# Spreading the next segment's projections over all head groups, with PSUM evictions moved from VectorE to ScalarE

## The chip, the cores and the metric

The kernel runs on one core of a Trainium2 chip. The metric is device time in microseconds. Five engines work side by side, each through its own list of instructions in order: TensorE (PE: matmuls, and PEld: its weight loads), VectorE (DVE), ScalarE (ACT), GpSimd (POOL) and SyncE (SP, which here only starts transfers). Matmul results land in PSUM, eight banks of 2 KB per partition, from which DVE or ACT must copy ("evict") them to SBUF before the bank can be used again.

## The reference

The input x has 2048 rows of 640 numbers, and 32 heads of 20 columns. Two attention layers read the same x, and a gate per row mixes them:

```
A: q,k,v = x@wqkv;  pq = q@w_phi, pk = k@w_phi              (per head)
   phi_q = [softmax(pq), softmax(-pq)],  phi_k likewise
   a = (phi_q @ (phi_k^T v)) / (phi_q . sum(phi_k) + 1e-6) @ wo
B: q,k,v = x@wq, x@wk, x@wv, cut into 4 segments of 512 rows
   per segment s: p = softmax(q k^T / sqrt(20) + causal mask); dot = p @ v
                  mem = (phi(q) @ M) / (phi(q) . z + 1e-6)    phi(t) = t+1 if t>0 else exp(t)
                  o = sigmoid(beta)*mem + (1-sigmoid(beta))*dot
                  M += phi(k)^T v;  z += sum(phi(k))
   b = o @ wo
out = sigmoid(x . gate_w) * a + (1 - that) * b
```

All inputs and the output are bf16. Segment s of B reads the memory M that the segments before it have written; inside a segment only 512 x 512 causal scores per head are made.

## The kernel before

**Stages.** (1) Weights and x are loaded, x is transposed into xT. (2) Stage A1, 16 chunks of 128 rows: project k and v of layer A, exp with both signs (Ek), reduce, normalise (EkSn), transpose EkSn into PSUM (zt_ps, one tile per sign, two slots) and copy both tiles to ztsb. The first copy is on DVE (line 222), the second on ACT (line 223). DVE then adds up zacc from ztsb, 32 small additions for every four chunks. (3) A2 builds the key-value matrices of layer A. (4) A3 computes layer A's queries and output into oA. (5) Stage B, lines 405 to 647, which the change rewrites. The A stages other than line 222 are untouched.

**Stage B.** The loops run over 4 segments (s) and in each over 8 groups (g) of 4 heads. Four heads of 20 columns, padded to 32 each, fill the 128 partitions. For each segment there is a set of three tiles, phik, vB and kpad, in a pool of two sets. `alloc_seg_tiles` takes a set and zeroes its padding with four memsets on DVE (lines 420 to 423); it is called at the start of segment s for segment s+1, so four times in all.

`emit_b1` (line 426) fills a quarter of a set, one chunk of 128 rows: 20 matmuls into four PSUM tiles `proj` (k in two halves, v in two halves), two exps on ACT into ek, then on DVE a minimum, two copies to kpad (445), two combinations into phik (447) and two copies to vB (453).

A group does the following. `emit_proj` makes qT (5 matmuls, eviction on DVE) and, from segment 1 on, phiq (exp eq on ACT). `emit_kT` transposes kpad. `emit_qk` is called four times, c = 0 to 3: four matmuls into st_ps, one exp on ACT over 4 x (512 - 128 c) columns into PT (498), a mask on DVE (499). `emit_pv` multiplies PT with vB into nd_ps, `emit_mem` does the memory read and update, `emit_epi` normalises and writes oB. The source order is software-pipelined inside a segment: while group g makes its scores, the qT and kT of group g+1 and the rest (`prev`) of group g-1 are done.

Filler is emitted between groups: in groups 4 to 7 one whole `emit_b1` for the next segment per group, and from segment 1 on the output product of the segment before, one chunk of rows per two groups (`final_part1`, ten transposes, in even groups; `final_part2`, twenty matmuls o_ps, in odd ones). At the end of each segment the last group is finished (mem, pv, epi) before the next segment's memsets, first qT and first kT are emitted. The last segment's four output chunks come after everything.

**PSUM in B.** st_ps has one tile of four banks, nd_ps one bank, and one tag, ps1, has three slots of a bank each for all the rest: proj, qT_ps, kT_ps, amS, Mz, ndS, otp and o_ps.

**What sets the order.** Each engine executes a list in fixed order. The list is not quite the order of the source: a planner goes through the emitted instructions, takes those emitted earlier first where they are ready by its estimate, and inserts the waits. So the source order acts as a priority.

Of the kernel before, what the change touches and what calls it, by code (L numbers as in the profile page):

```python
# [7 lines left out]
ACT = mybir.ActivationFunctionType  # L8
# [7 lines left out]
def kernel(  # L16
# [16 lines left out]
    P = 128  # L33
# [145 lines left out]
    with tc.tile_pool(name="a1work", bufs=2, side="right") as a1w, \  # L179
# [4 lines left out]
        for sc in range(NCH):  # L184
# [37 lines left out]
            nc.vector.tensor_copy(out=ztsb[0:ZR, 0, :, sc % 4, :], in_=zts[0][0:ZR])  # L222
# [182 lines left out]
    with ExitStack() as bctx:  # L405
# [4 lines left out]
        bseg = bctx.enter_context(tc.tile_pool(name="bseg", bufs=2))  # L410
# [4 lines left out]

        def alloc_seg_tiles():
            phik = bseg.tile([P, 4, H, 32], BF16, name="phik")
            vB = bseg.tile([P, 4, H, 32], BF16, name="vB")
            kpad = bseg.tile([P, 4, H, 32], BF16, name="kpad")
            nc.vector.memset(kpad[:, :, :, DH:32], 0.0)  # L420
            nc.vector.memset(phik[:, :, :, DH:32], 0.0)
            nc.vector.memset(vB[:, :, :, DH + 1:32], 0.0)
            nc.vector.memset(vB[:, :, :, DH:DH + 1], 1.0)
            return phik, vB, kpad

        def emit_b1(tiles, sc, c):
            phik, vB, kpad = tiles
            pss = []
            for (Wr, lo) in ((None, 0), (None, 16), (WvB, 0), (WvB, 320)):
                ps = bps.tile([P, 320], F32, name="proj", tag="ps1")  # L430
                for cc in range(KC):
                    if Wr is None:
                        rhs = WkB[:, cc, lo * DH:(lo + 16) * DH]
                    else:
                        rhs = Wr[:, cc, lo:lo + 320]
                    nc.tensor.matmul(ps[:, 0:320], lhsT=xT[:, cc, sc * P:(sc + 1) * P], rhs=rhs,  # L436
                                     start=(cc == 0), stop=(cc == KC - 1))
                pss.append(ps)
            k0, k1, v0, v1 = pss
            ek = bw.tile([P, 2, 320], BF16, name="ek", tag="ek")  # L440
            nc.scalar.activation(out=ek[:, 0, :], in_=k0[:, 0:320], func=ACT.Exp)
            nc.scalar.activation(out=ek[:, 1, :], in_=k1[:, 0:320], func=ACT.Exp)
            nc.vector.tensor_scalar_min(out=ek, in0=ek, scalar1=1.0)
            for half, kp, vp in ((0, k0, v0), (1, k1, v1)):
                nc.vector.tensor_copy(out=kpad[:, c, half * 16:(half + 1) * 16, 0:DH],  # L445
                                      in_=kp[:, 0:320].rearrange("p (h d) -> p h d", d=DH))
                nc.vector.scalar_tensor_tensor(
                    out=phik[:, c, half * 16:(half + 1) * 16, 0:DH],
                    in0=kpad[:, c, half * 16:(half + 1) * 16, 0:DH],
                    scalar=0.0,  # L450
                    in1=ek[:, half, :].rearrange("p (h d) -> p h d", d=DH),
                    op0=ALU.max, op1=ALU.add)
                nc.vector.tensor_copy(out=vB[:, c, half * 16:(half + 1) * 16, 0:DH],
                                      in_=vp[:, 0:320].rearrange("p (h d) -> p h d", d=DH))

        seg_tiles = alloc_seg_tiles()
        for c in range(4):
            emit_b1(seg_tiles, c, c)
        for s in range(NSEG):
            phik, vB, kpad = seg_tiles  # L460
            nxt_tiles = alloc_seg_tiles() if s + 1 < NSEG else None
            def emit_proj(g):
                qT_ps = bps.tile([P, L], F32, name="qT_ps", tag="ps1")
                for cc in range(KC):
# [210 lines left out]
```

The softmax here doesn't subtract the row's maximum and nothing guards it: scores larger than these inputs give would overflow.

## Time and profile before

| | |
|---|---|
| runs | 578.66, 579.18, 574.02, 579.85 us; median 578.92 |
| profiled execution | 578.66 us, span of its instructions 576.9 us |
| mean granted TensorE clock | 0.893 |
| stage A1 (about) | 43 to 127 us of the span |
| opening of B, four chunks of proj | 224 to 242 us |
| segments 0, 1, 2, 3 of B, from first exp to first exp | 244.3, 322.6, 406.8, 492.3, end 556.5 us |
| tail | 556.5 to 576.9 us |

How to read it: a profile row "L498 ACT ACTIVATE PT<-st_ps ... x128 | 158.3, 1237 | 82.7 <-PE st_ps L494 81.5" is line 498 of the kernel, its engine, what it writes and reads, how often; then busy time in us and the mean duration of one in ns; then the idle time of that engine just before these instructions, and which instruction ended most of it. The chain of waits follows the work back from the last instruction, at each step to whatever released it. Durations overlap a little at their ends, so a sum of durations is slightly more than the time taken. "PEclk" is the TensorE clock that was granted, as a share of full speed.

### The profile page before, as it was taken

To read this page: it belongs to the slowest core of one execution; us is meant where nothing else is said; L and a number is where in the kernel's file an instruction comes from. 1 tells how busy PE (TensorE), PEld (TensorE's weight loads), DVE (VectorE), ACT (ScalarE), POOL (GpSimd) and SP (SyncE) were. 2 spreads that over 40 slices of the span, in tenths; PEclk is the share of its full clock that TensorE was granted. 3 is DMA by queue.
4 is the path that set the end of the run, shared out by engine and by line. 5 is a ranking of instruction groups with operands and counts; after the bars stand their busy time and mean duration, and the time that the engine had idled before them with its cause. 6 is when DMAs were issued, how large, how long until landed. Compare 5 with 4: busy or idle time off the path is not lost.

```text
span 576.9 us, 10001 instructions
## 1 busy us (share of the span) xinstructions
PE 450.3 (78%) x4021; PEld 269.5 (47%) x4054; DVE 430.7 (75%) x1186; ACT 306.8 (53%) x460; POOL 20.0 (3%) x24
## 2 busy tenths in 40 slices
PE   0798988956759985867878687887778888778887
PEld 0676765455435553533344343544343455344444
DVE  2379999999298879854587877867875878787841
ACT  1556766910535550255574567463676554677731
POOL 3020000000260000000000000000000000000000
PEclk9999997967998895967688999989997899799989
DMA  8300000000710000000000000000000000000001
GB/s 257 97 2 1 3 0 1 1 1 1 230 58 1 1 2 1 0 1 2 1 1 1 0 13 12 1 13 12 1 12 13 1 12 12 1 12 12 12 13 45
DMA packets 9045, 12.46 MB, mean 22 GB/s; under 512 B 1992, under 2 KB 8264, under 8 KB 9000
## 3 DMA queue, kind: packets, MB, share of 16 engines
q1 hardware_dynamic: 8056, 8.06, 4.3%
q0 software_dynamic: 800, 3.77, 1.9%
q8 instruction: 31, 0.51, 0.4%
q14 instruction: 14, 0.11, 0.1%
q10 hardware_dynamic: 144, 0.01, 0.0%
HBM read 9.21 MB, written 2.62 MB: 21 GB/s over the span
## 4 chain that ended last, share of the span: by engine, by line
DVE 42%; PE 40%; ACT 11%; issue 4%; DMA 3%; SPq 0%; ACTq 0%; DVEq 0%
PE o_ps L598 9%; PE proj L436 8%; ACT PT L498 7%; PE st_ps L494 5%; DVE zacc L230 4%; PE pq_ps L335 4%; DVE ndsb L520 3%; DVE PT L499 3%; DVE EkSn L203 3%; PE nd_ps L513 3%; PE qT_ps L465 3%; DVE ksum L199 3%; DMA wnat_k<-in_A_wqkv_dram 3%; PE ndS L561 2%; DVE qT L469 2%
## 5 line engine op out<-in xcount | busy, mean ns | idle before, releaser
L498 ACT ACTIVATE PT<-st_ps 128x2048 bf16<-128x2048 f32 (+3 forms) x128 | 158.3, 1237 | 82.7 <-PE st_ps L494 81.5
L499 DVE TENSOR_TENSOR PT<-PT,maskT 128x512 bf16<-128x512 bf16 x128 | 53.6, 420 | 31.3 <-ACT PT L498 30.1
L494 PE MATMUL st_ps<-qT,kT 32*128 32x256 bf16 (+3 forms) x512 | 49.0, 324 | 24.1 <-ACT PT L498 22.7
L513 PE MATMUL nd_ps<-PT,vB 128*32 128x256 bf16 (+3 forms) x512 | 46.4, 320 | 6.2 <-DVE PT L499 5.8
L494 PEld LDWEIGHTS <-kT 32*128 32x128 bf16 x512 | 18.4, 92 | 65.1 <-issue 60.8
L465 PE MATMUL qT_ps<-xT,WqB 128*128 128x512 bf16 x136 | 42.2, 402 | 7.5 <-DVE kT L486 2.0
L436 PEld LDWEIGHTS <-xT 128*128 128x128 bf16 x320 | 33.0, 110 | 26.8 <-issue 7.5
L335 PE MATMUL pq_ps<-xT,WqA 128*128 128x512 bf16 x153 | 40.1, 402 | 3.5 <-ACT dens L351 1.6
L338 ACT ACTIVATE Eq<-pq_ps 128x512 bf16<-128x512 f32 x32 | 19.1, 597 | 43.2 <-PE pq_ps L335 42.4
L598 PEld LDWEIGHTS <-oT 128*128 128x128 bf16 x320 | 32.6, 109 | 19.8 <-DVE oT L587 2.6
L189 PEld LDWEIGHTS <-xT 128*128 128x128 bf16 x320 | 31.6, 100 | 14.7 <-issue 2.1
L436 PE MATMUL proj<-WkB,xT 128*128 128x320 bf16 x160 | 33.1, 360 | 4.4 <-issue 4.1
L469 DVE CAST qT<-qT_ps 128x512 bf16<-128x512 f32 x32 | 22.3, 698 | 18.5 <-PE qT_ps L465 18.3
L598 PE MATMUL o_ps<-WoA,oT 128*128 128x320 bf16 x160 | 33.9, 344 | 1.4 <-DVE oT L587 1.4
L561 PE MATMUL ndS<-ident_b,ndsb 128*128 128x128 bf16 x128 | 14.9, 248 | 24.5 <-DVE ndsb L520 24.5
L230 DVE TENSOR_TENSOR zacc<-zacc,ztsb 80x256 bf16<-80x256 bf16 x128 | 31.0, 275 | 1.6 <-ACT ztsb L223 1.0
L598 PE MATMUL o_ps<-WoB,oT 128*128 128x320 bf16 x160 | 31.2, 331 | 0.2 <-DVE oT L587 0.2
L602 ACT CAST osb<-o_ps 128x320 bf16<-128x320 f32 x32 | 13.6, 424 | 32.6 <-PE o_ps L598 32.6
L436 PE MATMUL proj<-WvB,xT 128*128 128x320 bf16 x160 | 29.7, 327 | 1.0 <-DVE kpad L445 1.0
L520 DVE CAST ndsb<-nd_ps 128x512 bf16<-128x512 f32 x32 | 21.9, 686 | 9.9 <-PE nd_ps L513 9.6
L389 DVE TENSOR_TENSOR t<-num_ps,cs 128x480 f32<-128x480 f32 (+1 forms) x64 | 27.9, 473 | 0.3 <-PE num_ps L361 0.3
L513 PEld LDWEIGHTS <-vB 128*32 128x32 bf16 x512 | 19.2, 98 | 17.8 <-issue 8.9
(135 smaller groups left out, 822.1 us busy)
## 6 DMA issues: line engine op xcount, KB each, us to landing
out_dram<-osb SPq DMA_DIRECT2D x16, 160.0 KB, 1.8
x_nat<-in_A_x_dram POOLq DMA_DIRECT2D x1, 1280.0 KB, 11.3
x_nat<-in_A_x_dram SPq DMA_DIRECT2D x1, 1280.0 KB, 14.7
WvA<-in_A_wqkv_dram SPq DMA_DIRECT2D x1, 800.0 KB
wnat_k<-in_A_wqkv_dram SPq DMA_DIRECT2D x1, 800.0 KB, 14.9
wnat_q<-in_A_wqkv_dram POOLq DMA_DIRECT2D x1, 800.0 KB, 12.5
WoB<-in_B_wo_dram POOLq DMA_DIRECT2D x1, 800.0 KB, 5.4
wst<-in_B_wv_dram POOLq DMA_DIRECT2D x1, 800.0 KB, 7.5
```

The costliest lines, as they stand in the source:

```text
L189: nc.tensor.matmul(ps, lhsT=xT[:, c, sc * P:(sc + 1) * P], rhs=W[:, c, lo:hi], start=(c == 0), stop=(c == KC - 1))
L230: nc.vector.tensor_tensor(out=zacc[0:ZR, b4], in0=zacc[0:ZR, b4], in1=zt_tile[0:ZR, :, :, :, 4 * t:4 * t + 4], op=ALU.add)
L335: nc.tensor.matmul(pq_ps, lhsT=WqA[:, c, g * P:(g + 1) * P], rhs=xT[:, c, qt * L:(qt + 1) * L], start=(c == 0), stop=(c == KC - 1))
L436: nc.tensor.matmul(ps[:, 0:320], lhsT=xT[:, cc, sc * P:(sc + 1) * P], rhs=rhs, start=(cc == 0), stop=(cc == KC - 1))
L465: nc.tensor.matmul(qT_ps, lhsT=WqB[:, cc, 4 * g:4 * g + 4, :], rhs=xT[:, cc, s * L:(s + 1) * L], start=(cc == 0), stop=(cc == KC - 1))
L469: nc.vector.tensor_copy(out=qT, in_=qT_ps)
L494: nc.tensor.matmul(st_ps[:, i, 0:N], lhsT=kT[32 * i:32 * i + 32, c * P:(c + 1) * P], rhs=qT[32 * i:32 * i + 32, c * P:L], start=True, stop ...
L498: nc.scalar.activation(out=PT, in_=st_ps[:, :, 0:N], func=ACT.Exp, scale=SCALE_B)
L499: nc.vector.tensor_tensor(out=PT[:, :, 0:P], in0=PT[:, :, 0:P], in1=maskT[:, None, :].to_broadcast([P, 4, P]), op=ALU.mult)
L513: nc.tensor.matmul(nd_ps[32 * i:32 * i + 32, c * P:L], lhsT=vB[:, c, h, :], rhs=PTs[c][:, i, :], start=(c == 0), stop=(c == 3), tile_posit ...
L520: nc.vector.tensor_copy(out=ndsb, in_=nd_ps)
L598: nc.tensor.matmul(o_ps, lhsT=oTs[X][:, k5, :], rhs=Wo[:, k5, half * 320:(half + 1) * 320], start=(n == 0), stop=(n == 2 * KC - 1))
```

## The change

1. In A1 the first ztsb copy (line 222) goes from DVE to ACT, so both are on ACT.
2. In B, kpad and vB are evicted by ACT instead of DVE, in `emit_b1`. The function now can do one half of k or of v alone; the minimum and the two phik combinations stay on DVE and come with the second half of k.
3. Two sets of phik, vB and kpad are allocated and zeroed once, ahead of the first `emit_b1`, and reused in turn. Segment s+1 uses set (s+1) mod 2, whose padding is still zero from the start. Two of the four rounds of memsets go.
4. The loops over segments and groups become one loop over 32 groups. The qT and kT of the next segment's first group are emitted during the last group, and the last group's mem, pv and epi during the next segment's first group.
5. The next segment's projections are spread: in every group g one half of a chunk's work is emitted, k of chunk g/2 in even groups, v in odd ones, each in two pieces of five matmuls at different places of the group.
6. The output product is cut into three items a chunk (transposes, first half, second half), handed out one or two a group; one item (a second half) is left over at each segment and, in the end, goes behind the last group.

```
-            nc.vector.tensor_copy(out=ztsb[0:ZR, 0, :, sc % 4, :], in_=zts[0][0:ZR])
+            nc.scalar.copy(out=ztsb[0:ZR, 0, :, sc % 4, :], in_=zts[0][0:ZR])
...
-        bseg = bctx.enter_context(tc.tile_pool(name="bseg", bufs=2))
+        bseg = bctx.enter_context(tc.tile_pool(name="bseg", bufs=1))
...
+        def emit_b1(tiles, sc, c, parts=("k0", "k1", "v0", "v1")):
             phik, vB, kpad = tiles
...
+            for half in range(2):
+                if f"k{half}" in parts:
+                    ps = bps.tile([P, 320], F32, name="proj", tag="ps1")
...
+                    nc.scalar.activation(out=ek[:, half, :], in_=ps[:, 0:320], func=ACT.Exp)
+                    nc.scalar.copy(out=kpad[:, c, half * 16:(half + 1) * 16, 0:DH],
+                                   in_=ps[:, 0:320].rearrange("p (h d) -> p h d", d=DH))
+                    if half == 1:
+                        nc.vector.tensor_scalar_min(out=ek, in0=ek, scalar1=1.0)
...
+            for half in range(2):
+                if f"v{half}" in parts:
+                    ps = bps.tile([P, 320], F32, name="proj", tag="ps1")
...
+                    nc.scalar.copy(out=vB[:, c, half * 16:(half + 1) * 16, 0:DH],
+                                   in_=ps[:, 0:320].rearrange("p (h d) -> p h d", d=DH))
...
+        for _ in range(2):
+            sets.append(alloc_seg_tiles())
+        tiles_of = {0: sets[0]}
+        for c in range(4):
+            emit_b1(tiles_of[0], c, c)
+        NG = NSEG * G
...
+        for k in range(NG):
+            s, g = divmod(k, G)
...
+            PTs = [emit_qk(qT_c, kT_c, 0)]
+            if s + 1 < NSEG and g == 0:
+                tiles_of[s + 1] = sets[(s + 1) % 2]
+
+            def fill(j):
+                if s + 1 < NSEG:
+                    emit_b1(tiles_of[s + 1], 4 * (s + 1) + g // 2, g // 2,
+                            parts=(("k%d" if g % 2 == 0 else "v%d") % j,))
+
+            def run_fin():
+                if s == 0:
+                    return
+                nfin = 1 if (g % 2 == 1 or (g == 0 and s == 1)) else 2
+                for item in fin_items[:nfin]:
+                    run_final_item(item)
+                del fin_items[:nfin]
+
+            if s > 0 and g == 0:
+                fin_items += final_items(range(4 * (s - 1), 4 * s))
+            if k + 1 < NG:
+                s1, g1 = divmod(k + 1, G)
...
+                qT_n, phiq_n = emit_proj(s1, g1)
+                kT_n = emit_kT(tiles_of[s1], g1)
...
+                tm_p = emit_mem(tiles_of[prev[0]], prev[0], prev[1], prev[3])
+            PTs.append(emit_qk(qT_c, kT_c, 1))
...
+                emit_pv(tiles_of[prev[0]], prev[1], prev[2], [0, 1])
+            if g > 0:
+                run_fin()
+            else:
+                fill(0)
+            PTs.append(emit_qk(qT_c, kT_c, 2))
...
+                ndsb_p = emit_pv(tiles_of[prev[0]], prev[1], prev[2], [2, 3])
+            fill(0) if g > 0 else fill(1)
+            PTs.append(emit_qk(qT_c, kT_c, 3))
+            if g > 0:
+                fill(1)
...
+                emit_epi(prev[0], prev[1], ndsb_p, tm_p)
+            if g == 0:
+                run_fin()
+            prev = (s, g, PTs, phiq_c)
...
+        for item in fin_items + final_items(range(4 * (NSEG - 1), 4 * NSEG)):
+            run_final_item(item)
```

More of the change, by code (lines that the diff above doesn't have):

```diff
@@ L424, in alloc_seg_tiles @@
             return phik, vB, kpad
-        def emit_b1(tiles, sc, c):
+        class PVState:
+            nd = None
+            ek = None
+        def emit_b1(tiles, sc, c, parts=("k0", "k1", "v0", "v1")):
             phik, vB, kpad = tiles
[L428 to L454, printed above, removed]
@@ L638 @@
[L638 to L644 removed]
+                tm = bw.tile([P, 4, 4, DH], F32, name="tm")
+                nc.vector.tensor_tensor(out=tm, in0=amv[:, :, :, 0:DH],
+                                        in1=rdm.to_broadcast([P, 4, 4, DH]), op=ALU.mult)
```

364 lines of the change are left out of this document (185 added, 179 removed).

## The prediction

> **What bounds the kernel now.** I read the page's first and fourth part first: is there one full engine, and what is the chain that ended last made of?
>
> ```profile
> span 576.9 us, 10001 instructions
> PE 450.3 (78%) x4021; PEld 269.5 (47%) x4054; DVE 430.7 (75%) x1186; ACT 306.8 (53%) x460; POOL 20.0 (3%) x24
> DVE 42%; PE 40%; ACT 11%; issue 4%; DMA 3%; SPq 0%; ACTq 0%; DVEq 0%
> PE o_ps L598 9%; PE proj L436 8%; ACT PT L498 7%; PE st_ps L494 5%; DVE zacc L230 4%; PE pq_ps L335 4%; DVE ndsb L520 3%; DVE PT L499 3%; DVE EkSn L203 3%; PE nd_ps L513 3%; PE qT_ps L465 3%; DVE ksum L199 3%; DMA wnat_k<-in_A_wqkv_dram 3%; PE ndS L561 2%; DVE qT L469 2%
> ```
>
> No engine is full: PE 78%, DVE 75%, ACT 53%. The chain belongs to DVE and PE by turns, and its two largest lines are matmul groups, o_ps (9%) and proj (8%). In the loop over groups these are filler, work that no exp of the same group needs. So filler stands on the path, and one asks where. The windows view, cut by stage, answers. Each row is start and end, length, busy time of PE, PEld, DVE, ACT and POOL (with instructions), the granted PE clock, DMA.
>
> ```profile
> 43.00:127.00 84.00, 71.78 (x612) 50.62 (x612) 81.93 (x172) 54.66 (x127) 0.00 (x0) 0.91 0.00 1
> 224.00:242.00 18.00, 15.58 (x83) 8.89 (x83) 15.67 (x35) 3.50 (x8) 0.00 (x0) 0.79 0.00 1
> 244.30:278.70 34.40, 24.75 (x176) 11.38 (x178) 17.64 (x50) 19.79 (x16) 0.00 (x0) 0.70 0.00 1
> 278.70:322.60 43.90, 35.51 (x302) 18.89 (x304) 33.23 (x90) 23.85 (x27) 0.00 (x0) 0.84 0.00 1
> 322.60:353.20 30.60, 23.19 (x224) 12.39 (x226) 23.53 (x72) 22.54 (x24) 0.00 (x0) 0.94 0.02 7
> 353.20:406.80 53.60, 43.46 (x381) 24.61 (x384) 42.45 (x128) 27.27 (x33) 0.00 (x0) 0.97 0.03 10
> 406.80:440.70 33.90, 27.30 (x239) 14.36 (x240) 24.49 (x73) 23.48 (x25) 0.00 (x0) 0.85 0.02 6
> 440.70:492.30 51.60, 44.25 (x395) 25.51 (x398) 41.48 (x125) 27.81 (x35) 0.00 (x0) 0.97 0.03 11
> 492.30:524.20 31.90, 25.00 (x213) 12.54 (x216) 22.50 (x63) 22.63 (x24) 0.00 (x0) 0.84 0.02 6
> 524.20:556.50 32.30, 26.08 (x253) 14.38 (x256) 24.17 (x72) 22.75 (x23) 0.00 (x0) 0.89 0.05 16
> ```
>
> The first row is the A1 stage, where DVE is full (81.93 of 84). The second is the opening of B. The other eight are the four segments of B, each cut into groups 0 to 3 and groups 4 to 7. Segment 1 shows the pattern: its first half takes 30.6 us, its second 53.6, with the same number of exps. Only the second half holds the projections for the next segment and the change of segments.
>
> Why the second half is long is in the timeline, at one filled group and at the three changes of segment (the bracket is idle time before the instruction and what ended it).
>
> ```profile
> 359.33 1.53 PE L436 MATMUL proj<-WkB,xT 128*128 128x320 bf16 x10
> 361.79 0.85 PE L436 MATMUL proj<-WvB,xT 128*128 128x320 bf16 x5
> 364.04 1.88 ACT L498 ACTIVATE PT<-st_ps 128x2048 bf16<-128x2048 f32 x1 [2.71 <-PE st_ps L494]
> 317.78 1.23 DVE L422 MEMSET vB<- 128x1408 bf16 x1 [0.24 <-issue]
> 320.61 0.63 ACT L473 ACTIVATE eq<-qT 128x512 bf16<-128x512 bf16 x1 [6.94 <-DVE qT L469]
> 405.45 0.63 ACT L473 ACTIVATE eq<-qT 128x512 bf16<-128x512 bf16 x1 [5.19 <-DVE qT L469]
> 490.77 0.63 ACT L473 ACTIVATE eq<-qT 128x512 bf16<-128x512 bf16 x1 [4.38 <-DVE qT L469]
> ```
>
> PE works through a whole chunk of proj before the next group's scores, and the exp comes 2.71 us late. At the changes ACT is idle for 6.94, 5.19 and 4.38 us, 16.5 together, until the first qT of the new segment has been evicted; a memset of the segment after next runs on DVE just there. So B is bound by lumps and drains, not by an engine.
>
> **The change, part by part.** Durations by line:
>
> ```profile
> L222 DVE COPY ztsb<-zt_ps 80x1024 bf16<-80x1024 bf16 x16 | 10.8, 678 | 0.9 <-PE zt_ps L218 0.9
> L223 ACT COPY ztsb<-zt_ps 80x1024 bf16<-80x1024 bf16 x16 | 16.3, 1017 | 7.9 <-PE zt_ps L218 7.8
> L445 DVE CAST kpad<-proj 128x320 bf16<-128x320 f32 x32 | 15.5, 485 | 2.5 <-ACT ek L441 2.5
> L453 DVE CAST vB<-proj 128x320 bf16<-128x320 f32 x32 | 15.5, 485 | 2.0 <-PE proj L436 1.8
> L208 ACT CAST vAaug<-a1t 128x320 bf16<-128x320 f32 x16 | 7.0, 439 | 7.9 <-PE a1t L189 7.9
> L441 ACT ACTIVATE ek<-proj 128x320 bf16<-128x320 f32 x16 | 7.0, 437 | 22.9 <-PE proj L436 22.9
> L447 DVE SCALAR_TENSOR_TENSOR phik<-kpad,ek 128x320 bf16<-128x320 bf16 x32 | 15.2, 483 | 0.0
> L443 DVE TENSOR_SCALAR ek<-ek 128x640 bf16<-128x640 bf16 x16 | 5.2, 323 | 2.4 <-ACT ek L442 2.2 <-issue 0.2
> L422 DVE MEMSET vB<- 128x1408 bf16 x4 | 4.9, 1232 | 1.0 <-issue 1.0
> L420 DVE MEMSET kpad<- 128x768 uint32 x4 | 2.8, 698 | 0.6 <-DVE oA L393 0.2
> L602 ACT CAST osb<-o_ps 128x320 bf16<-128x320 f32 x32 | 13.6, 424 | 32.6 <-PE o_ps L598 32.6
> L598 PE MATMUL o_ps<-WoA,oT 128*128 128x320 bf16 x160 | 33.9, 344 | 1.4 <-DVE oT L587 1.4
> ```
>
> *A1: one ztsb copy of each chunk from DVE to ACT.* DVE loses 10.8 us (L222) and stands at 81.93 - 10.8 = 71.1; ACT gains 16 x 1.017 = 16.3 and stands at 54.66 + 16.3 = 71.0. Both would be near 71 of 84, and they feed each other: behind an ACT copy that waits for its transposes stand the next chunk's exps, for which DVE's reduction waits. Best case -10.8; worst case, where all 16.3 land on the path and only 10.8 leave it, +5.5. I take -5, about half of the best, since two coupled engines at 71 do not run to their sum.
>
> *Opening of B.* The 16 evictions of the first four chunks leave DVE (16 x 0.485 = 7.8) for ACT (16 x 0.44 = 7.0, by L208, the same shape and type on ACT); ACT has 3.50 of 18 in use. The second set's memsets, which lay between the evictions, now stand ahead of them: 0.70 + 0.70 (phik, of kpad's size) + 1.23 = 2.6 us of DVE. PE is busy 15.58 of 18, so at best 2.4 goes; at worst the memsets hold the first qT back, +2.6. I take -2: ACT, not DVE, now frees the projection's PSUM tiles.
>
> *The group loop.* PE's work is unchanged; what moves is its place. Per segment 0 to 2, eighty proj matmuls in four lumps become ten in each of eight groups: 1.53 us of PE a group, by the timeline row. ACT gets per chunk two ek, two kpad and two vB pieces, 6 x 0.44 = 2.6, or 1.3 a group, DVE min and phik, (0.32 + 2 x 0.48) / 2 = 0.64. Is there room? In groups 0 to 3 of segment 1 a group takes 30.6 / 4 = 7.65 us, with PE idle (30.6 - 23.19) / 4 = 1.85, ACT (30.6 - 22.54) / 4 = 2.0, DVE (30.6 - 23.53) / 4 = 1.8. So the fill just fits PE's gaps; hidden wholly it costs 0, not at all 1.53. I take half, 0.75, for segments 1 and 2. In segment 0 PE is idle (34.4 - 24.75) / 4 = 2.4 us and ACT 3.7 in a group of 34.4 / 4 = 8.6; I take a quarter, 0.4. Final pieces are as dense as in today's first halves of segments 1 to 3, one chunk to two groups, so they are in the pace.
>
> With today's first-half pace for all eight groups, and with no drain, because the next segment's qT and kT are now emitted in the group before and no memset is left in the loop:
> segment 0: 8 x (8.6 + 0.4) = 72.0, against 34.4 + 43.9 = 78.3: -6.3.
> Segment 1: 8 x (7.65 + 0.75) = 67.2, against 84.2: -17.0.
> Segment 2: 33.9 / 4 = 8.48, 8 x (8.48 + 0.75) = 73.8, against 85.5: -11.7.
> Segment 3 has no fill: 64.2 stays, 0.
> Together -35.0. What is late next is the exp itself: an ACT eviction ahead of an exp holds it, PE waits for its one st_ps tile, and 0.75 a group is the price put on that.
>
> *Tail.* One half chunk of finals (ten o_ps matmuls, 0.15 each by the proj row of the same shape, so 1.5) is left over behind the last group, its store with it on SP's queue, which then holds nothing else. It needs only the segment before, so a gap may take it: 0 to +1.5, I take +1.
>
> A rule that speaks against the change: the Trainium skill, "ScalarE: Activation LUTs", section "Rules for kernel authors", wants plain arithmetic on VectorE, which it puts at up to about three times ScalarE's speed per element in bf16. By that factor the 64 evictions would take 64 x 3 x 0.485 = 93 us of ACT and not 28, an estimate from that page by which the sum would end at about 603, if all of it lay on the path. The trace disagrees for this form (439 ns on ACT against 485 on DVE) and agrees in direction for the ztsb copy (1017 against 678), so I give this rule no chance of its own.
>
> Sum: -5 - 2 - 35.0 + 1 = -41. The profiled execution took 578.66 us (1.8 more than its span) and the median of the runs is 578.92, so one base serves: 578.7 - 41 = 537.7, say **538**.
>
> **The rivals.**
> *The fill is not hidden.* PE and ACT have only 1.85 and 2.0 us to spare a group, in pieces between QK and exp. If each group pays all 1.53, segments 0 to 2 give 8 x (1.13 + 0.78 + 0.78) = 21.5 back: 559. For it: proj and o_ps are on today's chain of waits. Against: those are lumps of ten and twenty, and pieces of five are 0.85 us. Chance 0.20.
>
> *The order on the engines doesn't follow the source.* The planner has already regrouped work:
>
> ```profile
> 307.75 0.76 PE L513 MATMUL nd_ps<-PT,vB 128*32 128x512 bf16 x16
> L498 ACT ACTIVATE PT<-st_ps 128x2048 bf16<-128x2048 f32 (+3 forms) x128 | 158.3, 1237 | 82.7 <-PE st_ps L494 81.5 <-DVE PT L499 0.8
> ```
>
> The source splits these sixteen matmuls eight and eight around a score step. If it lumps the fills again, only the drains go (-16.5) and the opening's 2, while 48 evictions in the loop land on ACT's path, 48 x 0.44 = +21: 578.7 + 2.5 = 581, no change that counts. Chance 0.08.
>
> *Slower: PSUM slots held behind the exps.* The fill's tiles share three ps1 slots with qT, kT, amS, Mz, ndS and the finals. DVE drained them at once; on ACT a tile can wait behind an exp of 1.237 us on average (L498). If PE stalls for all of it at each of the 48 tiles, that is +59, against the -41: 597. It decides from 41 / 48 = 0.85 us a tile. For it: ACT runs in order and its exps are long. Against: o_ps is drained by ACT from the same slots today, and its group shows 1.4 us of PE idle in 160 matmuls, waiting for oT, not for ACT; ACT waits for PE there (32.6 us, L602). Chance 0.08.
>
> **How the numbers follow.** Forecast as summed 0.62, fill exposed 0.20, regrouped 0.08, slots 0.08, and 0.02 for better than all bounds. The forecast's own range: fill wholly hidden gives -(8 x (0.4 + 0.75 + 0.75)) = -15.2, and A1 at its best -5.8; I count one of them whole and part of the other, 519. At the other end A1 +5.5 instead of -5 is +10.5, the opening +4.6: 553. The fill-exposed case with half of A1's loss, 559 + 5, sets the upper end, 564. What a measurement here can tell from no change is about 1%, 573 to 585. Faster: 0.62 + 0.20 + 0.02 = 0.84; within 1%: 0.08; slower: 0.08.
>
> A side gain that is not in the sum: the clock is granted at 0.70 in segment 0's first half and 0.97 in the filled second half of segment 1. Denser PE work in segment 0 could bring its pace nearer to 7.65, at most 8 x 0.95 = 7.6 us, one more reason for the low end. The Trainium skill, "TensorE: Matmul & The Clock Gate", section "Part 1", says the throttled state is the default and activity lifts it, which the two rows bear out.
>
> **What would show it.** Right: the first and second halves of a segment take the same time; ACT's idle before eq at the changes of segment falls below 1.5 us; no proj run in the loop is longer than five or ten matmuls; the A1 row is near 79 us with DVE and ACT about equal; ACT's busy total is near 306.8 + 28 + 16 = 351 and DVE's near 430.7 - 31 - 11 - 5 = 384. Wrong: PE idle on ACT evictions of proj (slots), exps idle as long before st_ps as now, 81.5 us in all (regrouped), or a second half that is still longer than the first (fill exposed). If A1 grows, the first step fails by itself, whatever B does.

## The result, and the profile after

The changed kernel takes 514.25 us (median of 11 runs, 510.98 to 516.40); the kernel before takes 579.45 us in the runs beside it (median of 16). The ratio is 0.889, with a 95% interval from 0.885 to 0.893. The direction was forecast, the size was not: 538 was predicted, and 514 lies below the low end of the range, 519.

The profiled execution after took 511.77 us, with a span of 509.9, so the span lost 67.0. The first lines of its page, the chain's two parts last:

```profile
span 509.9 us, 10009 instructions
PE 426.1 (84%) x4015; PEld 256.9 (50%) x4054; DVE 390.2 (77%) x1098; ACT 336.8 (66%) x540; POOL 19.8 (4%) x24
PE 47%; DVE 35%; ACT 10%; issue 4%; DMA 3%; SPq 0%; ACTq 0%
PE o_ps L602 9%; PE nd_ps L519 7%; PE proj L461 5%; DVE zacc L230 5%; PE pq_ps L335 5%; PE st_ps L500 5%; DVE ksum L199 4%; PE qT_ps L470 4%; DVE EkSn L203 4%; ACT PT L504 3%; DMA wnat_k<-in_A_wqkv_dram 3%; PE proj L439 3%; DVE ndsb L526 2%
```

PE now holds the larger share of the chain, 47% against 40%, and its busy total *fell* from 450.3 to 426.1 us though its work is the same. A busy total that falls with the work unchanged says that the same matmuls ran shorter. The windows show where. This view of the changed kernel has the same columns as in the prediction (start and end, length, busy time of PE, PEld, DVE, ACT, POOL, granted clock, DMA): the A1 stage, the opening of B, the halves of segments 0, 1 and 2, and segment 3 with the tail in three pieces.

```profile
43.00:117.00 74.00, 65.08 (x598) 45.53 (x598) 73.21 (x156) 65.73 (x142) 0.00 (x0) 1.00 0.01 1
212.60:230.50 17.90, 16.71 (x99) 10.12 (x101) 12.39 (x25) 8.81 (x24) 0.00 (x0) 0.84 0.00 1
230.50:261.00 30.50, 26.24 (x232) 13.15 (x235) 20.17 (x57) 24.74 (x32) 0.00 (x0) 1.00 0.00 1
261.00:291.30 30.30, 25.55 (x234) 12.53 (x237) 21.86 (x63) 24.66 (x31) 0.00 (x0) 1.00 0.01 1
291.30:323.70 32.40, 30.58 (x289) 16.48 (x294) 26.32 (x80) 25.31 (x33) 0.00 (x0) 1.00 0.02 7
323.70:355.30 31.60, 30.22 (x292) 17.50 (x293) 27.13 (x87) 26.69 (x37) 0.00 (x0) 1.00 0.03 11
355.30:390.30 35.00, 33.53 (x309) 18.72 (x313) 28.96 (x91) 27.56 (x37) 0.00 (x0) 1.00 0.03 11
390.30:423.80 33.50, 32.21 (x308) 18.62 (x312) 28.59 (x90) 27.25 (x36) 0.00 (x0) 1.00 0.03 11
423.80:456.00 32.20, 28.02 (x267) 15.42 (x270) 26.81 (x79) 23.27 (x25) 0.00 (x0) 0.95 0.03 11
456.00:488.00 32.00, 25.82 (x251) 13.69 (x250) 25.51 (x74) 22.66 (x23) 0.00 (x0) 0.95 0.03 12
488.00:509.90 21.90, 16.96 (x134) 11.89 (x134) 5.30 (x13) 3.83 (x9) 0.00 (x0) 0.92 0.10 38
```

The two halves of each of segments 0 to 2 are now equal within 1.5 us, and the granted clock is 1.00 in all six halves of segments 0 to 2. In segment 0's first half more matmuls (232 against 176) took less time (30.5 against 34.4 us), at clock 1.00 instead of 0.70. In segments 1 and 2 PE is busy for 94 to 96% of each half: by its busy share, an engine is now close to full there. (The counts are of recorded matmuls; a few are missing in every trace.)

By stage, in us. A1 is taken from the first to the last start of EkSn (L203), the opening from the start of the last oA to the first exp, and segment 3 includes the tail; what lies between A1 and the opening did not move.

| stage | before | after | change | forecast |
|---|---|---|---|---|
| A1 | 73.6 | 63.5 | -10.3, with what precedes it | -5 |
| opening of B | 21.3 | 17.9 | -3.4 | -2 |
| segment 0 | 78.3 | 60.8 | -17.5 | -6.3 |
| segment 1 | 84.2 | 63.9 | -20.3 | -17.0 |
| segment 2 | 85.5 | 68.5 | -17.0 | -11.7 |
| segment 3 and tail | 84.6 | 86.1 | +1.5 | +1 |
| sum | | | -67.0 | -41 |

The miss is 26.0 us: segment 0 has 11.2 of it, A1 5.3, segment 2 5.3, segment 1 3.3, the opening 1.4, and the tail takes 0.5 back.

Groups of the changed kernel that answer to those shown of before (busy, mean ns of one, idle time ahead and what ended it); the first line is that of eq in the kernel before:

```profile
L473 ACT ACTIVATE eq<-qT 128x512 bf16<-128x512 bf16 x24 | 15.0, 627 | 19.3 <-DVE qT L469 19.2
L504 ACT ACTIVATE PT<-st_ps 128x2048 bf16<-128x2048 f32 (+3 forms) x128 | 158.7, 1240 | 40.0 <-PE st_ps L500 38.3
L478 ACT ACTIVATE eq<-qT 128x512 bf16<-128x512 bf16 x24 | 15.0, 626 | 3.4 <-DVE qT L474 3.1
L446 ACT CAST kpad<-proj 128x320 bf16<-128x320 f32 x32 | 14.1, 439 | 0.0
L464 ACT CAST vB<-proj 128x320 bf16<-128x320 f32 x32 | 13.8, 431 | 6.5 <-PE proj L461 6.5
L461 PE MATMUL proj<-WvB,xT 128*128 128x320 bf16 x160 | 29.6, 312 | 0.5 <-ACT vB L464 0.5
L222 ACT COPY ztsb<-zt_ps 80x1024 bf16<-80x1024 bf16 x16 | 16.8, 1050 | 1.0 <-DVE zacc L230 1.0
```

The exps cost what they did (1240 ns against 1237), but their idle time before st_ps fell from 81.5 to 38.3 us, and that of eq from 19.2 to 3.1 in all. PE waited 0.5 us for an ACT eviction of vB at L461 (its row) and 0.5 us at L439, both in the opening of B; in the loop it never waited for an eviction of kpad or vB.

The timeline of the changed kernel, in one filled group of segment 0 and at the change to segment 1:

```profile
257.59 0.43 PE L439 MATMUL proj<-WkB,xT 128*128 128x320 bf16 x2
258.54 1.12 PE L439 MATMUL proj<-WkB,xT 128*128 128x320 bf16 x7
259.22 0.43 ACT L445 ACTIVATE ekp<-proj 128x320 bf16<-128x320 f32 x1
259.53 0.43 ACT L446 CAST kpad<-proj 128x320 bf16<-128x320 f32 x1
259.77 0.31 PE L439 MATMUL proj<-WkB,xT 128*128 128x320 bf16 x1
261.00 1.91 ACT L504 ACTIVATE PT<-st_ps 128x2048 bf16<-128x2048 f32 x1
...
291.34 1.88 ACT L504 ACTIVATE PT<-st_ps 128x2048 bf16<-128x2048 f32 x1
```

The ten matmuls of this group go in runs of two, seven and one, and the next exp (261.00) is not late. In a few other groups the planner put eight to ten of them in one run. The first exp of segment 1 (291.34) follows without idle time where 6.94 us stood before.

### The profile page after: what moved, and what is told of

Read it like the earlier page. It is cut to its first block, busy times and chain, and to the rows that moved or that the text cites. A ratio compares the mean times of both kernels' runs of the same rounds, so it can differ in the third digit from the quotient of the medians.

```text
span 509.9 us, 10009 instructions
## 1 busy us (share of the span) xinstructions
PE 426.1 (84%) x4015; PEld 256.9 (50%) x4054; DVE 390.2 (77%) x1098; ACT 336.8 (66%) x540; POOL 19.8 (4%) x24
## 4 chain that ended last, share of the span: by engine, by line
PE 47%; DVE 35%; ACT 10%; issue 4%; DMA 3%; SPq 0%; ACTq 0%
PE o_ps L602 9%; PE nd_ps L519 7%; PE proj L461 5%; DVE zacc L230 5%; PE pq_ps L335 5%; PE st_ps L500 5%; DVE ksum L199 4%; PE qT_ps L470 4%; DVE EkSn L203 4%; ACT PT L504 3%; DMA wnat_k<-in_A_wqkv_dram 3%; PE proj L439 3%; DVE ndsb L526 2%; DVE PT L505 2%; PE ndS L567 2%
## 5 line engine op out<-in xcount | busy, mean ns | idle before, releaser
L504 ACT ACTIVATE PT<-st_ps 128x2048 bf16<-128x2048 f32 (+3 forms) x128 | 158.7, 1240 | 40.0 <-PE st_ps L500 38.3
L505 DVE TENSOR_TENSOR PT<-PT,maskT 128x512 bf16<-128x512 bf16 x128 | 53.2, 416 | 19.0 <-ACT PT L504 18.3
L519 PE MATMUL nd_ps<-PT,vB 128*32 128x256 bf16 (+3 forms) x512 | 58.8, 306 | 2.1 <-DVE PT L505 1.6
L500 PE MATMUL st_ps<-qT,kT 32*128 32x256 bf16 (+3 forms) x512 | 41.4, 304 | 6.0 <-ACT PT L504 5.5
L470 PE MATMUL qT_ps<-xT,WqB 128*128 128x512 bf16 x130 | 38.7, 380 | 2.6 <-issue 1.6
L189 PEld LDWEIGHTS <-xT 128*128 128x128 bf16 x320 | 30.6, 98 | 15.6 <-issue 4.5
L519 PEld LDWEIGHTS <-vB 128*32 128x32 bf16 x512 | 24.8, 96 | 24.9 <-issue 9.9
L439 PE MATMUL proj<-WkB,xT 128*128 128x320 bf16 x160 | 28.4, 312 | 4.7 <-issue 4.1
L602 PE MATMUL o_ps<-WoA,oT 128*128 128x320 bf16 x160 | 29.9, 310 | 1.2 <-DVE oT L593 1.2
L230 DVE TENSOR_TENSOR zacc<-zacc,ztsb 80x256 bf16<-80x256 bf16 x128 | 30.5, 273 | 0.6
L526 DVE CAST ndsb<-nd_ps 128x512 bf16<-128x512 f32 x32 | 22.0, 688 | 11.3 <-PE nd_ps L519 11.2
L461 PE MATMUL proj<-WvB,xT 128*128 128x320 bf16 x160 | 29.6, 312 | 0.5 <-ACT vB L464 0.5
L189 PE MATMUL a1t<-WvA,xT 128*128 128x320 bf16 (+1 forms) x160 | 25.6, 300 | 3.0 <-ACT Ek L196 3.0
L335 PEld LDWEIGHTS <-WqA 128*128 128x128 bf16 x160 | 15.8, 102 | 24.2 <-issue 10.9
L593 DVE COPY oT<-otp 128x640 bf16<-128x640 bf16 x32 | 14.6, 487 | 14.4 <-PE otp L590 14.2
## 6 DMA issues: line engine op xcount, KB each, us to landing
x_nat<-in_A_x_dram POOLq DMA_DIRECT2D x1, 1280.0 KB, 11.2
```

What stands on the lines that cost most here:

```text
L189: nc.tensor.matmul(ps, lhsT=xT[:, c, sc * P:(sc + 1) * P], rhs=W[:, c, lo:hi], start=(c == 0), stop=(c == KC - 1))
L230: nc.vector.tensor_tensor(out=zacc[0:ZR, b4], in0=zacc[0:ZR, b4], in1=zt_tile[0:ZR, :, :, :, 4 * t:4 * t + 4], op=ALU.add)
L335: nc.tensor.matmul(pq_ps, lhsT=WqA[:, c, g * P:(g + 1) * P], rhs=xT[:, c, qt * L:(qt + 1) * L], start=(c == 0), stop=(c == KC - 1))
L470: nc.tensor.matmul(qT_ps, lhsT=WqB[:, cc, 4 * g:4 * g + 4, :], rhs=xT[:, cc, s * L:(s + 1) * L], start=(cc == 0), stop=(cc == KC - 1))
L500: nc.tensor.matmul(st_ps[:, i, 0:N], lhsT=kT[32 * i:32 * i + 32, c * P:(c + 1) * P], rhs=qT[32 * i:32 * i + 32, c * P:L], start=True, stop ...
L504: nc.scalar.activation(out=PT, in_=st_ps[:, :, 0:N], func=ACT.Exp, scale=SCALE_B)
```

## The experiments

Four of the kernels undo one part each, three test the clock, one makes one part alone in the kernel before, and one takes a step further. The question above all: why did segment 0, where almost nothing was wrong by the forecast but the lumps in its second half, gain 17.5 us? Three answers were open: the evictions' engine, the order of the fill, and the clock. What a kernel loses or gains against the changed one is taken from the two ratios, and by their intervals each such difference is uncertain by 2 to 4 us; what a stage loses is taken from the profiled executions.

**The ztsb copy back on DVE, in the changed kernel.**

```
-            nc.scalar.copy(out=ztsb[0:ZR, 0, :, sc % 4, :], in_=zts[0][0:ZR])
+            nc.vector.tensor_copy(out=ztsb[0:ZR, 0, :, sc % 4, :], in_=zts[0][0:ZR])
```

> The changed kernel with only the A1 step undone: the first ztsb copy is on DVE again. If A1 is bound by DVE alone, the stage goes back from 74 to about 84 us and the whole by +10 (504 to 514 becomes about 524). If, as the prediction priced it, ACT and DVE bind each other and half of DVE's saving is lost, the step is worth only about 5, and another part of the change must have shortened A1.

Measured: 523.1 us, ratio 0.904 (0.900 to 0.909), so 0.0154 of 579, 8.9 us, is lost. A1 takes 73.8 us again, and the segments stay within 1.6 us of what they were. The windows view of this kernel, A1:

```profile
44.20:127.20 83.00, 70.89 (x605) 49.62 (x603) 80.83 (x166) 54.54 (x127) 0.00 (x0) 0.92 0.00 1
```

DVE is busy 80.83 of 83.0, and 73.21 of 74.0 without these sixteen copies: it is full both times, so what is taken off DVE comes off the stage. ACT at 65.73 of 74 does not hold it back.

**The kpad and vB evictions back on DVE, in the changed kernel.** The rest of the projection's order stays.

```
-                    nc.scalar.copy(out=kpad[:, c, half * 16:(half + 1) * 16, 0:DH],
+                    nc.vector.tensor_copy(out=kpad[:, c, half * 16:(half + 1) * 16, 0:DH],
...
-                    nc.scalar.copy(out=vB[:, c, half * 16:(half + 1) * 16, 0:DH],
+                    nc.vector.tensor_copy(out=vB[:, c, half * 16:(half + 1) * 16, 0:DH],
```

> The changed kernel with kpad and vB evicted by DVE again, in the opening and in the loop; the spreading, the joined segments and the single memsets stay. Theory clock (the spread projections keep PE dense, the granted clock rises to 1.00, and that hides the fill): 0 to +5 us, the groups of segment 0 stay near 7.6 us and the clock at 1.00. Theory queue (the gain beyond the forecast comes from DVE's shorter queue, so that qT, masks and ndsb are out sooner): +12 to +24 us, half to one us a group.

Measured: 523.1 us, ratio 0.904 (0.900 to 0.909): 8.8 us lost. That is more than the clock's 0 to 5 and less than the queue's 12 to 24. By stage the opening loses 5.0, segment 0 only 0.35, segment 1 1.3, segment 2 1.8. The windows of this kernel, opening and first half of segment 0:

```profile
217.20:239.30 22.10, 17.33 (x98) 10.21 (x97) 18.00 (x40) 3.50 (x8) 0.00 (x0) 0.74 0.00 1
239.30:269.80 30.50, 26.27 (x233) 12.97 (x232) 23.48 (x66) 21.66 (x22) 0.00 (x0) 1.00 0.01 2
```

In segment 0 the evictions' engine makes no difference: 30.5 us and clock 1.00 either way. More than half of what this part of the change is worth lies in the opening, where DVE has 18.0 of 22.1 us to do and ACT 3.5. The waits view of this kernel's opening (in total, times, longest) shows PE standing still for one kpad:

```profile
PE proj L461 <- DVE kpad L446: 4.4, 1, 4.4
```

**The fill whole, at the ends of four groups.** All else of the change stays: no memset in the loop, the next segment's qT and kT a group ahead, evictions on ACT.

```
             def fill(j):
-                if s + 1 < NSEG:
+                if False:
...
+            if s + 1 < NSEG and 3 <= g <= 6:
+                emit_b1(tiles_of[s + 1], 4 * (s + 1) + (g - 3), g - 3)
```

> The changed kernel with the fill lumped again: one whole chunk of twenty proj matmuls at the end of each of groups 3 to 6, none in the others; ACT evictions, joined segments and single memsets stay. Theory clock: segment 0's first groups are thin again, the clock there falls to 0.7 to 0.85 and they take 8 to 8.6 us in place of 7.6; the lumps cost about 1.5 us each in all three segments; together +20 to +30. Theory queue: only the lumps cost, 12 x 1 to 1.5 us, +12 to +18, and the first groups of segment 0 get faster than 7.6, since they hold less work.

Measured: 533.6 us, ratio 0.921 (0.915 to 0.927): 18.3 us lost; in the profiled execution 4.9 in segment 0, 8.3 in segment 1, 6.9 in segment 2. Segment 0 in this kernel's windows: the first half, then its groups 0 to 2 and its group 3, and the second half:

```profile
233.50:269.00 35.50, 28.35 (x194) 12.45 (x195) 17.71 (x48) 21.65 (x22) 0.00 (x0) 0.66 0.00 1
233.50:259.00 25.50, 19.17 (x138) 8.26 (x141) 13.36 (x37) 14.85 (x12) 0.00 (x0) 0.66 0.00 1
259.00:269.00 10.00, 9.18 (x60) 4.19 (x60) 4.36 (x11) 6.80 (x10) 0.00 (x0) 0.68 0.01 2
269.00:299.20 30.20, 26.44 (x269) 14.59 (x272) 23.41 (x65) 26.07 (x36) 0.00 (x0) 1.00 0.01 1
```

Spreading is the largest single part, though not clearly larger than the next. But the loss in segment 0 doesn't follow the lumps: the second half, with three of the four, takes 30.2 us at clock 1.00. The first half, with fewer matmuls than in the changed kernel (194 against 232), takes 5.0 us longer, at clock 0.66. Half of that is lost before the first lump: groups 0 to 2, which hold no fill here, take 25.5 us, and 22.9 with the fill in the changed kernel. The rest is lost in group 3, at whose end the first lump stands (10.0 us against 7.6, at clock 0.68); what lump and clock cost there can't be parted. So the first groups got slower with less work, which the theory of queues alone does not give; the total of 18.3 lies just above its 12 to 18 and just below the clock's 20 to 30. In segments 1 and 2 the lumps do cost, at clock 1.00.

**Segments separated again.** The last group of a segment is finished before the next segment's qT and kT are made; spread fill and ACT evictions stay.

```
-            if k + 1 < NG:
+            if g + 1 < G:
...
+            if g == G - 1 and s + 1 < NSEG:
+                tm_p = emit_mem(tiles_of[s], s, g, phiq_c)
+                emit_pv(tiles_of[s], g, PTs, [0, 1])
+                ndsb_p = emit_pv(tiles_of[s], g, PTs, [2, 3])
+                emit_epi(s, g, ndsb_p, tm_p)
+                prev = None
+                qT_n, phiq_n = emit_proj(s + 1, 0)
+                kT_n = emit_kT(tiles_of[s + 1], 0)
```

> The changed kernel with the segments separated again: the last group is finished and only then the next segment's first qT and kT are emitted; no memsets there. If the drain itself cost the 16.5 us that ACT was idle at the three changes, +12 to +17 us. If the memsets at those places were the cause, +0 to +4.

Measured: 529.8 us, ratio 0.916 (0.911 to 0.920): 15.5 us lost; in the profiled execution 6.5 in segment 0, 6.2 in segment 1, 1.5 in segment 2. From this kernel's timeline, the first eq of segment 1:

```profile
300.27 0.63 ACT L478 ACTIVATE eq<-qT 128x512 bf16<-128x512 bf16 x1 [6.12 <-DVE qT L474]
```

In the windows of this kernel, the second half of segment 0:

```profile
265.10:300.00 34.90, 25.44 (x231) 12.86 (x231) 20.47 (x59) 22.38 (x25) 0.00 (x0) 0.91 0.01 1
```

The wait of before is back (6.12 us, 6.94 then) with no memset in the loop, and the clock, 1.00 in the first half, falls to 0.91 in the half that holds it. So the drain is the order of emission, and the memset, which in the kernel before stood just there, was not what made it.

**No fill in segment 0: less work.** Segment 0 projects nothing, and segment 1 attends with segment 0's keys and values; so the projections for segment 1 are left out.

```
-                tiles_of[s + 1] = sets[(s + 1) % 2]
+                tiles_of[s + 1] = sets[s % 2]
...
-                if s + 1 < NSEG:
+                if 0 < s and s + 1 < NSEG:
```

> The changed kernel without the projections for segment 1: segment 0 has no fill at all, and segment 1 computes with segment 0's keys and values in place of its own (the output of segments 1 to 3 is another). 80 proj matmuls, 48 ACT pieces and their DVE work are gone. Theory clock: segment 0 becomes thin on PE, the granted clock falls to about 0.7 and its eight groups take 8 to 8.6 us in place of 7.6, so with less work the whole is 3 to 8 us slower than the changed kernel. Theory room (the fill is free merely because the gaps have room for it): the groups keep 7.6 us or fall toward 7, the whole is 0 to 5 us faster.

Measured: 525.5 us, ratio 0.905 (0.903 to 0.908). With 80 matmuls and all their evictions gone the kernel is 9.3 us *slower* than with them. Segment 0 takes 72.3 us instead of 60.8; the other stages are within 1.5 us of the changed kernel's. Its halves of segment 0:

```profile
235.70:270.70 35.00, 26.46 (x186) 11.55 (x186) 17.98 (x50) 19.85 (x17) 0.00 (x0) 0.66 0.00 1
270.70:308.00 37.30, 29.80 (x208) 13.25 (x207) 19.98 (x57) 22.09 (x22) 0.00 (x0) 0.68 0.00 1
```

No engine is near full, nothing is in lumps, and the granted clock averages 0.66 and 0.68. The loss is larger than the clock's forecast of 3 to 8 us, as the groups take 9.0 us and not 8 to 8.6. The first half's 186 matmuls keep PE busy for 26.46 us, where the changed kernel's 232 took 26.24: each runs longer, so scores and PV products come later. Theories that speak only of lumps and queues give a segment 0 no longer than 60.8 here.

**The same, with unread matmuls at the places of the fill.**

```
             def fill(j):
-                if 0 < s and s + 1 < NSEG:
+                if s == 0:
+                    dm = bps.tile([P, 320], F32, name="dum", tag="ps1")
+                    for cc in range(KC):
+                        nc.tensor.matmul(dm, lhsT=xT[:, cc, 0:P], rhs=WkB[:, cc, 0:320],
+                                         start=(cc == 0), stop=(cc == KC - 1))
+                elif s + 1 < NSEG:
```

> The run without the projections for segment 1, again with segment 0's keys and values in segment 1, but with sixteen runs of five matmuls that nobody reads at the very places of the missing fill in segment 0; ACT and DVE get none of the fill's work. Theory clock: PE's density alone counts, so the clock in segment 0 goes from 0.67 back to about 1.00, its eight groups from 72 to 56 to 61 us, and the whole from 525 to 509 to 515. If the order that the fill's ACT and DVE pieces force is what helps, segment 0 stays at 70 to 77 us and the whole at 523 to 530.

Measured: 513.9 us, ratio 0.887 (0.882 to 0.892), by the ratios 10.4 us less than without the unread matmuls; segment 0 takes 60.4 us, as in the changed kernel. Its halves:

```profile
233.40:263.20 29.80, 26.06 (x230) 13.17 (x232) 18.07 (x50) 19.80 (x17) 0.00 (x0) 1.00 0.00 1
263.20:293.80 30.60, 25.58 (x236) 12.97 (x242) 20.14 (x57) 21.98 (x23) 0.00 (x0) 1.00 0.01 1
```

Eighty matmuls whose result nobody reads, in sixteen runs of five, lift the mean clock from 0.66 and 0.68 to 1.00. What the fill computes has no part in it, nor have its evictions: added work on PE is enough.

**Unread matmuls in the kernel before.** Two runs of five in each of groups 0 to 3 of segments 0 and 1, behind the two halves of the PV product.

```
+            def dummy():
+                if s < 2 and g < 4:
+                    dm = bps.tile([P, 320], F32, name="dum", tag="ps1")
+                    for cc in range(KC):
+                        nc.tensor.matmul(dm, lhsT=xT[:, cc, s * P:(s + 1) * P], rhs=WkB[:, cc, 0:320],
+                                         start=(cc == 0), stop=(cc == KC - 1))
```

> The kernel before with eighty added matmuls whose results nobody reads: two runs of five in each of groups 0 to 3 of segments 0 and 1, at the places where the change puts its fill; PE work alone, no eviction. Theory clock: segment 0's first half gets shorter with more work, from 34.4 to 30 to 31 us, as its clock goes from 0.70 to about 1.00; segment 1's first half, which stood at 0.94, gets 0 to 3 us longer; the whole between -4 and +1. Theory room: both halves get up to 6 us longer, the whole +4 to +12.

Measured: 571.7 us, ratio 0.982 (0.975 to 0.989): the kernel before gets faster by useless work. The first half of segment 0 and both halves of segment 1 in this kernel:

```profile
245.60:275.10 29.50, 24.41 (x221) 12.41 (x219) 17.76 (x50) 19.79 (x17) 0.00 (x0) 1.00 0.00 1
316.70:347.00 30.30, 27.83 (x271) 15.17 (x270) 23.81 (x72) 22.74 (x24) 0.00 (x0) 1.00 0.02 7
347.00:405.10 58.10, 48.21 (x385) 26.27 (x384) 43.10 (x128) 27.40 (x34) 0.00 (x0) 0.88 0.03 9
```

Segment 0's first half falls from 34.4 to 29.5 us. In segment 1, where the clock stood at 0.94 already, 40 more matmuls cost that half nothing (30.3 against 30.6): the gaps hold them. But the second half of segment 1, whose instructions are those of before, takes 58.1 us at clock 0.88 where it took 53.6 at 0.97, and segments 2 and 3, also unchanged, are 2.9 and 0.9 us shorter. The clock of stages that nobody touched moved too, so the whole gain, by the ratio 10 us and more than the forecast -4 to +1, is not all the doing of the stage that the matmuls were put in. What this kernel shows by itself is segment 0's first half.

**The kpad and vB evictions on ACT, alone, in the kernel before.**

```
-                nc.vector.tensor_copy(out=kpad[:, c, half * 16:(half + 1) * 16, 0:DH],
+                nc.scalar.copy(out=kpad[:, c, half * 16:(half + 1) * 16, 0:DH],
...
-                nc.vector.tensor_copy(out=vB[:, c, half * 16:(half + 1) * 16, 0:DH],
+                nc.scalar.copy(out=vB[:, c, half * 16:(half + 1) * 16, 0:DH],
```

> The kernel before with only kpad and vB evicted by ACT; lumps, drains, memsets and A1 as before. Undoing this step in the changed kernel cost 5 us in the opening and about 3 in the loop. If the step stands for itself, -5 to -9 here too. If it needs the spreading (four tiles at once wait for ACT behind an exp, and PE stalls for ps1 slots), nothing or a few us of loss in the loop: -5 to +3.

Measured: ratio 0.968 (0.962 to 0.975), 18 us less than before, twice what the same edit is worth inside the changed kernel and outside both forecasts (-5 to -9, and -5 to +3). In the profiled execution the opening gives 4.4 of it (16.9 us against 21.3). That execution (566.28 us) is the longest of the four, so the loop's stages are not read from it, and why the edit gives more where the fill is in lumps stays open.

**A step further: layer A's half of the last output product into segment 3.** In the changed kernel segment 3 has no fill, its clock is 0.95, and behind it stand the last four chunks' finals. Half of each needs only layer A's output, long there. It goes to the empty places of the fill; the partial sum is kept in bf16 in the free tile set and added by DVE at the end. The lines below are the changed places in the loop and behind it; the bodies of the new functions, and the line that runs the left-over item in the last group, are not shown.

```
+                elif g % 2 == 0:
+                    emit_oA(g // 2, "tr" if j == 0 else 0)
+                elif j == 0:
+                    emit_oA(g // 2, 1)
...
-        for item in fin_items + final_items(range(4 * (NSEG - 1), 4 * NSEG)):
+        for item in fin_items:
             run_final_item(item)
+        for ci in range(4):
+            final_B(ci)
```

> The changed kernel with the half of the last four chunks' output product that needs only layer A (five transposes and ten o_ps matmuls a chunk) moved from the tail into segment 3's empty fill places, kept in bf16 in a set that is free by then, and added on DVE in the tail; the left-over item goes into the last group. Theory clock: segment 3, at a clock of 0.95 and PE busy 54 of 64 us, takes it at no cost, and the tail loses 4 x 1.6 us and the left-over 1.5: -5 to -8 against the changed kernel. Theory room: segment 3 pays what the tail saves, -2 to +2.

Measured: 510.3 us, ratio 0.879 (0.876 to 0.882), 6.1 us under the changed kernel by the ratios, and the fastest of all. Segment 3 with the tail takes 80.35 us instead of 86.1. Its windows, the halves of segment 3 and the tail:

```profile
429.60:461.60 32.00, 30.94 (x299) 17.26 (x298) 27.43 (x79) 24.82 (x29) 0.00 (x0) 1.00 0.03 12
461.60:490.00 28.40, 27.38 (x272) 15.46 (x269) 23.76 (x66) 23.84 (x27) 0.00 (x0) 1.00 0.05 19
490.00:509.90 19.90, 11.13 (x92) 6.89 (x89) 9.98 (x27) 0.85 (x2) 0.00 (x0) 0.89 0.09 33
```

Segment 3's first half holds 32 more matmuls than in the changed kernel and is no longer (32.0 against 32.2); its clock went from 0.95 to 1.00. (The span of its profiled execution is 509.9 too: there A1 began 2.4 us later. That start moves between 45.6 and 49.5 us from one profiled execution to another, so only lengths of stages are compared here.)

## Why the prediction was right and wrong

**What bounds the kernel: right, but not the whole.** Lumps and drains were named, and both cost. The third bound, the clock in segment 0, was named only beside the sum; part of what lumps and drains cost comes through it, as the clock falls in segment 0 when either is put back (0.66 and 0.91). With the lumps back 18.3 us go, with the drains back 15.5, with the evictions back on DVE 8.8, with the ztsb copy back 8.9. That is 51.5 of 64 us (0.111 of 579), each part undone alone and uncertain by 3 to 4 us. The rest was not measured apart; the memsets taken out of the loop and what the parts do for each other are in it.

**A1, "-5, about half of the best, since two coupled engines at 71 do not run to their sum": the step failed.** Here they ran to the larger of the two. DVE alone set the stage, the copy left it, and nearly the whole 10.8 came off (10.1 between the first and the last EkSn, and 73.8 - 63.5 = 10.3 by the copy put back). The row for the prediction, 79 with both engines equal, came out as 74 with DVE at 73.21 and ACT at 65.73. The prediction's row had the answer: 81.93 of 84 is a full engine, and ACT had 29 us to spare.

**Opening, -2: too small by 1.4.** The best case, -2.4, was taken from PE's 15.58 of 18 us as a floor. The stage fell to 17.9 us from the last oA (21.3 before), and with the evictions back on DVE it is 22.9, 4.4 of which PE waits for one kpad on DVE. So DVE's evictions, not PE alone, set it. With the evictions on ACT and nothing else changed the stage takes 16.9, so the rest of the change costs 1.0 here; the memsets now ahead of the evictions are the likely cause, and were not measured alone. Nor was PE's busy time a floor: over the whole stage it fell from 18.74 us at clock 0.80 to 16.71 at 0.84.

**Group loop, segment 0, "8 x (8.6 + 0.4) = 72.0": the step that failed most, by 11.2.** The 8.6 was the pace of a half at clock 0.70, and the step kept that pace and put work on top. Measured is 7.60 a group, fill included: 8 x (8.6 - 7.60) = 8.0 for the pace, 8 x 0.4 = 3.2 for the fill, which costs nothing against the old pace. (What an unfilled group would take at the full clock no run shows.) The kernel without fill in segment 0 takes 72.3 us, the one with unread matmuls in its place 60.4: so the fill did not only fit in, it is what made the pace. The 0.70 was an average: in finer windows the kernel before reads 1.00 and 0.50 by turns in this stretch, while the changed kernel reads 1.00 throughout.

```profile
244.30:248.70 4.40, 2.71 (x23) 1.38 (x21) 2.80 (x9) 3.57 (x3) 0.00 (x0) 1.00 0.00 0
248.70:258.90 10.20, 7.94 (x49) 3.32 (x50) 4.67 (x13) 5.36 (x5) 0.00 (x0) 0.50 0.01 2
258.90:262.40 3.50, 1.78 (x24) 0.99 (x24) 1.54 (x3) 2.67 (x3) 0.00 (x0) 0.99 0.00 0
262.40:265.80 3.40, 3.18 (x17) 1.41 (x17) 1.42 (x5) 1.37 (x2) 0.00 (x0) 0.50 0.00 0
265.80:269.20 3.40, 2.12 (x21) 1.02 (x19) 2.56 (x8) 1.87 (x4) 0.00 (x0) 1.00 0.01 2
```

The prediction had this as "a side gain that is not in the sum, at most 7.6 us", a good size, and gave it no case and no lower end. A mechanism with a price of 7.6 us and a row to bear it out belonged in the sum with a chance of its own.

That gain stands beside a rule: the Trainium skill, "TensorE: Matmul & The Clock Gate", section "Why this matters for your kernels", asks for no PE idle longer than about 3 us to keep the clock up. By that rule alone the clock, which was up at 244.3, would have stayed up here, and the trace differs: in the kernel before PE's longest wait from 244.3 to 278.7 us was 0.9 us, while the granted clock averaged 0.70. The waits view of before, in that stretch (in total, times, longest):

```profile
PE st_ps L494 <- ACT PT L498: 4.7, 10, 0.9
PE ndS L561 <- DVE ndsb L520: 2.5, 3, 0.8
```

The Trainium skill, "TensorE: Matmul & The Clock Gate", section "A second HAM failure mode: psum-queue depth-cycling", tells of a kernel in which frequent short idles between groups of matmuls made the clock swing between half and full. The trace agrees: the five rows above swing between 0.50 and 1.00, with no wait over 0.9 us.

**Segments 1 and 2, "0.75" a group for exposed fill: mis-sized.** Segment 1 took 63.9 us, 7.99 a group, so against the old pace the price was 7.99 - 7.65 = 0.34; the clock rose there too, from 0.94 to 1.00, so at an equal clock it may be more. Segment 2 took 8.56 a group, where the step had 8.48 + 0.75; but 8.48 was a pace at clock 0.85 and the clock is now 1.00, so pace and price can't be parted there. Both segments have PE busy for 94 to 96%, which neither the sum nor a rival had. That PE now bounds them is read from this share alone; no run tested it.

**Segment 3, 0, and the tail, +1: right** (+1.5 together).

**The rivals.** Fill not hidden (559) falls: 0.34 a group in segment 1, nothing in segment 0, against 1.53. The planner regrouping (581) falls: runs of two, seven and one in the group shown, and no idle at the change. Its sum also leaves out A1's -5, which the planner's order in B doesn't touch; by the prediction's own terms it is 576. PSUM slots held behind the exps (597) falls: PE waited 1.0 us in all for ACT's evictions of vB, none of it in the loop. Of the ACT total forecast, 351, only 336.8 came, though the new rows add up to 16.8 + 14.1 + 13.8 = 44.7 us; the prediction added durations to a busy total, and ACT's instructions overlap in the timeline (259.22 and 259.53, each 0.43 long). All of ACT's rows add up to 326.5 us before and 377.1 after, 20 and 40 us over the busy totals, so the total grew by less than the rows.

## What to carry to other kernels

Before a thin stretch's pace is used as the base of a forecast, read its granted clock: where it is well under 1.00 with short gaps, work moved into the gaps can cost less than nothing, and the pace of a dense stretch of the same kernel (here 7.65 a group) was the better estimate. Where one engine was busy for 97% of a stage and its partner for two thirds, work moved from the one to the other was worth nearly its full duration (10.1 to 10.3 of 10.8 us); halving it for fear of coupling needs a row that shows the coupling. And where no useful work is at hand for the gaps, ten unread matmuls a group were here a cheap way to see what the clock is worth.

## What was not expected of the hardware

The granted clock averaged 0.66 to 0.70 over stretches of 34 to 37 us while PE was busy for 72 to 80% of them and never waited for another engine for more than 1.0 us. The waits view of the kernel without fill, over its segment 0 (in total, times, longest):

```profile
PE st_ps L500 <- ACT PT L504: 7.3, 16, 1.0
PE ndS L567 <- DVE ndsb L526: 5.7, 7, 0.8
```

With ten more matmuls a group it stayed at 1.00, and PE's busy time did not rise (26.46 us with 186 matmuls, 26.06 with 230, in halves of 35.0 and 29.8 us). In two kernels, useless matmuls took about 10 us off the time, by the ratios. What exactly the clock follows is not shown. PE's busy share alone doesn't sort the stretches: segment 1's first half in the kernel before had PE busy for 76% at clock 0.94, and the kernel without fill, in the first half of its segment 0, for 76% at 0.66. Nor does the longest wait: the changed kernel, at clock 1.00, waited up to 1.0 us too.

ACT's own instructions in A1 got longer when more of them stood there: Ek (L196) went from 451 to 495 ns, the ztsb copy of line 223 from 1017 to 1060. No run tested why.
